# Attention with normed q and k, then a gated feed-forward net: rearranging the outset, the order of the weights' sums, and the place of three conversions

## The chip, the cores and the metric

The kernel runs on one core of one Trainium2 chip. The metric is the device time in microseconds (us) of one execution, given as the median of several. Besides that I use the trace of one profiled execution of each kernel: its instructions with start, duration and what ended the wait ahead of them, and the granted clock of TensorE.

## The reference

```python
# q, k, v: (8, 12, 448, 64) float32; w_gate, w_val: (768, 1536); w_out: (1536, 768)
def rmsnorm(x, g): return x / sqrt(mean(x * x, -1) + 1e-6) * g
scores = rmsnorm(q, g_q) @ rmsnorm(k, g_k).T / 8          # per head
attn   = softmax(scores) @ v                              # (8, 12, 448, 64)
x      = attn.transpose(0, 2, 1, 3).reshape(3584, 768)
xn     = rmsnorm(x, rms_g)
g      = xn @ w_gate
out    = (g * sigmoid(g) * (xn @ w_val)) @ w_out
```

## The kernel before

The kernel goes through 8 sequences of 6 pairs of heads. While the attention of one pair runs, TensorE's pauses are filled with products of the feed-forward net of the sequence before. Each head's 448 rows are 3 tiles of 128 and a "rest" of 64 rows; the rests of several pairs are normed together. From sequence 1 on, the weights are used in a Strassen form, which needs sums of weight blocks: 72 of one kind (`derive`) and some of a second kind (`derive_o`), all made on VectorE. In the first sequence the weights are converted (`convert`: each one goes through ScalarE, then VectorE, then GpSimd). Names in the traces: `tr` are transposes, `sc` scores, `e` exponentials, `den` denominators and `rd` their reciprocals, `av` products with v and `x` = `av` times `rd`, `rb` the reciprocal roots of x's rows spread over a bank, `ff` the feed-forward products, `p` and `u` copies and sums that empty their banks (a bank is a piece of the memory that TensorE writes to), `w` a block of weights or a sum of two (`top` in some places), `warm` products of the identity. In source order the emitter calls `pe(...)` for one step of TensorE; `after(n, ...)` puts work n steps later. Cuts are marked with `# ...`.

```python
def norm_rests(b, lo, hi):
    n = hi - lo
    rest = st["rest", b][:, lo:hi]
    # ... square on ScalarE, then after(1): row sums on VectorE into ms
    def scale():
        nc.gpsimd.tensor_scalar(ms, ms, D * 1e-6, None, ALU.add)
        nc.gpsimd.tensor_tensor(ms, ms, mhalf[...], ALU.pow)          # reciprocal roots
        nc.gpsimd.tensor_tensor(rest, rest, ms..., ALU.mult)
    after(1 if b == 0 else 2, scale)

def norm_q(g):                                                        # qn = q * rs
    for h in range(2):
        nc.gpsimd.tensor_tensor(qn..., st["qk", g]..., st["rs", g]..., ALU.mult)

def fill(n=None):
    # ... for each step of the feed-forward net that is due:
        while asked["derived"] < sums_made:      # a sum that this step needs
            derive(0)                            # ...
        pe(fn)
        convert()
        derive()
        derive()
        derive_o()

# the outset
squares(0, 0); warm(9)                           # warm(n): n products of the identity
norm_rests(0, 0, 1)                              # pair 0's rest
# ... turn(0, 1), squares of pair 1
warm(3)
pe(lambda: turn(0, 0))                           # transposes of q, and of the rest
norm_rests(0, 1, 3)                              # rests of pairs 1 and 2
# ... g == 0: scores of pair 0, squares of pair 2, turn(1, 0), turn(1, 1)
# ... each later pair of the first sequence: convert() in three slots
```

The exponentials of a pair are added up by GpSimd (`es`, for the denominators) soon after the pair's scores.

## Time and profile before

| | before |
|---|---|
| median (range), us | 1622.38 (1621.83 to 1622.67) |
| span of the profiled execution, us | 1619.2 |
| TensorE busy | 98% |
| TensorE idle in 0 to 20 / 320 to 460 / 460 to 1400 us | 8.8 / 8.6 / 1.3 |
| half clock (granted clock 0.5), us from the start | 19.6 to 26.4, 347.2 to 350.7, 449.6 to 453.1 |

TensorE is the bound; what a change can win is idle time of TensorE and time at half clock. The main lines stand in the prediction below. TensorE's waits in 85 to 103 us (engine, line, releaser: total us, how often, longest):

```profile
PE av L563 <- issue: 1.9, 1, 1.9
```

### The profile page before, as it was taken

Reading aid. Unit: us, or ns where it says so; the run is one execution under the profiler, and the core shown is the slowest. Engines: PE = TensorE matmul, PEld = TensorE weight load, DVE = VectorE, ACT = ScalarE, POOL = GpSimd, SP = SyncE. Lnnn points to the kernel's source line nnn. Section 1 sums busy time; section 2 is a strip of 40 time slices with the busy share of each in tenths; the row PEclk is TensorE's granted clock in tenths of the full one; section 3 lists DMA queues with packets and bytes.
Section 4 is the critical chain, followed back from the end, with each engine's and each line's share of the span. In section 5 each row is a group of like instructions: output and inputs, shape, how many; then the busy total and the mean of one; then the engine's idle time right before and its main releaser. Section 6 shows DMA issues by size and latency. Waiting matters only on the chain.

```text
span 1619.2 us, 21550 instructions
## 1 busy us (share of the span) xinstructions
PE 1587.8 (98%) x7328; PEld 1124.6 (69%) x7328; DVE 864.3 (53%) x1490; ACT 471.7 (29%) x944; POOL 649.3 (40%) x672
## 2 busy tenths in 40 slices
PE   7999999999999999999999999999999999999998
PEld 3344445677865888668875688758886588969974
DVE  4989899378852354425563354524565235433431
ACT  5746564223221232223222222222232123101110
POOL 6867877444523344324632444334443322100000
PEclk9999999999999999999999999999999999999999
DMA  6747574566665655575544655476454464557652
GB/s 190 220 137 251 173 237 138 188 196 223 199 221 162 187 147 156 158 222 153 154 142 132 195 153 160 118 224 186 141 156 127 147 181 114 153 187 234 173 144 58
DMA packets 264586, 276.81 MB, mean 171 GB/s; under 512 B 79124, under 2 KB 261396, under 8 KB 264468
## 3 DMA queue, kind: packets, MB, share of 16 engines
q1 hardware_dynamic: 263540, 275.15, 56.3%
q8 instruction: 60, 0.98, 0.3%
q14 instruction: 58, 0.48, 0.1%
q10 hardware_dynamic: 800, 0.20, 0.1%
q0 software_dynamic: 128, 0.00, 0.0%
HBM read 235.93 MB, written 39.32 MB: 170 GB/s over the span
## 4 chain that ended last, share of the span: by engine, by line
PE 80%; DVE 6%; issue 0%; ACT 0%; POOL 0%; DVEq 0%; ACTq 0%
PE ff L878 39%; PE ff L1076 21%; PE av L579 5%; PE sc L527 5%; PE ff L973 3%; PE sc L557 2%; PE den L592 2%; PE tr L511 1%; DVE rd L600 1%; DVE w L835 1%; DVE top L726 1%; DVE top L727 1%; PE ff L1107 0%; DVE w L855 0%; DVE top L725 0%
## 5 line engine op out<-in xcount | busy, mean ns | idle before, releaser
L878 PE MATMUL ff<-x,w 128*128 128x224 f32 x1704 | 350.6, 355 | 3.0 <-ACT p L911 3.0
L878 PEld LDWEIGHTS ff<-x,w 128*128 128x128 f32 x1704 | 321.3, 191 | 14.6 <-issue 5.9
L537 POOL TENSOR_TENSOR es<-e 128x448 f32<-128x448 f32 x82 | 91.3, 1134 | 525.5 <-ACT e L531 525.5
L878 PE MATMUL ff<-xs,w 128*128 128x224 f32 x1320 | 272.0, 354 | 1.0 <-DVE u L890 1.0
L878 PEld LDWEIGHTS ff<-xs,w 128*128 128x128 f32 x1320 | 248.7, 191 | 5.4 <-issue 3.9
L1076 PE MATMUL ff<-w,h 128*128 128x384 f32 x582 | 200.2, 487 | 0.0
L544 POOL TENSOR_TENSOR es<-es,e 64x448 f32<-64x448 f32 (+1 forms) x164 | 194.1, 1194 | 6.3
L600 DVE RECIPROCAL rd<-rd 128x448 f32<-128x448 f32 x41 | 121.0, 2952 | 126.6 <-ACT rd L599 126.5
L531 ACT ACTIVATE e<-sc,rs 128x448 f32<-128x448 f32 x288 | 161.6, 634 | 50.6 <-PE sc L527 48.7
L1076 PEld LDWEIGHTS ff<-w,h 128*128 128x128 f32 x582 | 109.0, 190 | 76.1 <-DMA vt<-in_v_dram 3.3
L527 PE MATMUL sc<-qT,kT 64*128 64x448 f32 x576 | 138.7, 575 | 3.4 <-DVE kT L517 2.1
L1076 PE MATMUL ff<-w,so 128*128 128x384 f32 x350 | 120.4, 488 | 2.0 <-DVE y L1037 2.0
L579 PE MATMUL av<-e,vt 128*64 128x448 f32 x576 | 119.3, 549 | 0.0
L490 POOL TENSOR_TENSOR rs<-ms,mhalf 128x12 f32<-128x12 f32 (+1 forms) x50 | 114.9, 2298 | 4.2
L527 PEld LDWEIGHTS sc<-qT,kT 64*128 64x128 f32 x576 | 54.4, 186 | 84.0 <-issue 68.3
L1107 PE MATMUL ff<-x,w 128*128 128x448 f32 x288 | 111.8, 541 | 0.0
L890 DVE TENSOR_TENSOR cc<-ff,u 128x448 f32<-128x448 f32 x84 | 52.3, 623 | 88.9 <-PE ff L878 88.8
L1076 PEld LDWEIGHTS ff<-w,so 128*128 128x128 f32 x350 | 65.5, 190 | 48.4 <-DVE y L1037 3.9
L763 POOL TENSOR_TENSOR w<-top,raw 128x384 int32<-128x384 int32 x72 | 77.0, 1083 | 39.4 <-DVE top L727 24.2
L579 PEld LDWEIGHTS av<-e,vt 128*64 128x64 f32 x576 | 37.2, 137 | 76.6 <-issue 75.9
L1107 PEld LDWEIGHTS ff<-x,w 128*128 128x128 f32 x288 | 53.3, 190 | 50.8 <-issue 49.0
L613 POOL TENSOR_TENSOR ss<-ss,rd 128x448 f32<-128x448 f32 x40 | 47.4, 1185 | 76.9 <-ACT rd L612 76.9
(122 smaller groups left out, 1912.8 us busy)
## 6 DMA issues: line engine op xcount, KB each, us to landing
w<-kept SPq DMA_DIRECT2D x477, 192.0 KB, 2.9
w<-kept_o SPq DMA_DIRECT2D x290, 192.0 KB, 2.8
kept<-w SPq DMA_DIRECT2D x86, 192.0 KB, 3.9
top<-kept SPq DMA_DIRECT2D x75, 192.0 KB, 2.5
qk<-in_q_dram SPq DMA_DIRECT2D x48, 192.0 KB, 2.9
qk<-in_k_dram SPq DMA_DIRECT2D x96, 96.0 KB, 3.3
vt<-in_v_dram SPq DMA_DIRECT2D x48, 192.0 KB, 2.5
raw<-in_moe_w_gate_dram SPq DMA_DIRECT2D x24, 384.0 KB, 4.6
```

The lines of the kernel that those rows point to most:

```text
L490: nc.gpsimd.tensor_tensor(st["rs", g][:, cols], ms, mhalf[:, cols], ALU.pow)
L527: nc.tensor.matmul(ps[:, 0:S], lhsT=kT[r, c * 128:(c + 1) * 128], rhs=qT[r, :], start=True, stop=True)
L531: nc.scalar.activation(e, ps[:, 0:S], ACT.Exp, scale=rs[:, n:n + 1])
L537: nc.gpsimd.tensor_tensor(es, st["e", g, 0, j], st["e", g, 1, j], ALU.add)
L544: nc.gpsimd.tensor_tensor(es[r], es[r], e[r], ALU.add)
L579: nc.tensor.matmul(av[own(j), 0:S], lhsT=vt[:, j, c], rhs=st["e", g, c, j], start=False, stop=(c == NK - 1), skip_group_check=True)
L600: nc.vector.reciprocal(rd, rd)
L763: nc.gpsimd.tensor_tensor(data(key).bitcast(I32), top, lo, ALU.add)
L878: nc.tensor.matmul(bank[:, w * HT:(w + 1) * HT], lhsT=wt[:, c * 128:(c + 1) * 128], rhs=x[:, c, :], start=onto is None and w == c == 0, st ...
L890: nc.vector.tensor_tensor(add[name], ps[:, 0:S], add[other], ALU.add)
L1076: nc.tensor.matmul(ps, lhsT=a, rhs=data(("wo", b, name, c)), start=first and c == 0, stop=c == NFP - 1, skip_group_check=True)
L1107: nc.tensor.matmul(bank[w][:, 0:S], lhsT=data(key)[:, c * 128:(c + 1) * 128], rhs=st["x", 0, half][:, c, :], start=half == c == 0, stop=ha ...
```

## The change

Its intent: in the outset, norm the rests of pairs 0 and 1 in one group, put q's scaling of the first two pairs and the first rest's on VectorE, and fill two pauses with seven more products of the identity so that the clock stays up; in sequence 1, hold the weights' sums back while GpSimd adds exponentials, then make up to five a step; in the last pair of the first sequence, move three conversions behind the denominators and the scores.

```diff
 def norm_rests(b, lo, hi):
+    first = b == lo == 0
     def root():  # add and pow on GpSimd
+    def scale():
+        (nc.vector if first else nc.gpsimd).tensor_tensor(rest, rest, ms..., ALU.mult)
+    after(1 if b == 0 else 2, root)
+    if first:
+        return scale
 def norm_q(g):
-            nc.gpsimd.tensor_tensor(qn...)
+            (nc.vector if g <= 1 else nc.gpsimd).tensor_tensor(qn...)
 def turn(g, i):                       # q: between its transposes and the rest's
+            if g == 0:
+                warm(5)
 def fill(n=None):
-            derive()
-            derive()
-            derive_o()
+            if now["t"] - st["block"] > 4:       # steps since the pair's scores
+                for _ in range(3):
+                    derive()
+                derive_o()
+                derive_o()
 # outset
-    norm_rests(0, 0, 1)
+    scale = norm_rests(0, 0, 2)
+    after(1, scale)                   # behind squares(0, 1)
-    warm(3)
+    warm(5)
-    norm_rests(0, 1, 3)
 # g == 0 (pair 1's transposes now around the squares of pair 2)
+            norm_rests(0, 2, 4)
 # pairs 1 to 6: the three slots for conversions
-            convert() / convert() / convert()
+            turns(g < NPAIR) / turns(g < NPAIR) / turns(1 if g < NPAIR else 3)
```

## The prediction

> **What bounds the kernel now.** I read the page's busy shares and slices, then the table of windows, the list of TensorE's waits, and the timeline around each wait.
>
> ```profile
> PE 1587.8 (98%) x7328; PEld 1124.6 (69%) x7328; DVE 864.3 (53%) x1490; ACT 471.7 (29%) x944; POOL 649.3 (40%) x672
> ...
> PE   7999999999999999999999999999999999999998
> ```
>
> TensorE is busy nearly everywhere; the comparison of instruction orders shows that the change leaves TensorE's order alone except for seven more identity products. So the change can only win back idle stretches and stretches of half clock. The table of windows (busy us by engine, then granted clock) says where these are:
>
> ```profile
> 0.00:20.00 20.00, 11.20 (x54) 7.47 (x54) 5.17 (x15) 10.77 (x21) 14.73 (x30) 0.99 0.80 216
> 19.00:27.00 8.00, 6.57 (x22) 1.96 (x24) 3.48 (x8) 3.79 (x9) 5.54 (x6) 0.57 0.45 115
> ...
> 320.00:460.00 140.00, 131.38 (x681) 108.85 (x680) 112.16 (x198) 36.68 (x73) 60.24 (x61) 0.98 0.67 217
> ...
> 460.00:1400.00 940.00, 938.70 (x4517) 698.21 (x4517) 430.34 (x757) 247.42 (x487) 350.50 (x358) 1.00 0.54 161
> ```
>
> From 460 on there is 1.3 us to win in 940, and the change touches nothing there. The outset has 8.8 us without a matmul in 20, followed by half clock (0.57 over 8 us, so about 6.9 us at half). Sequence 1's products, 320 to 460, have 8.6 us idle; narrow windows there show 0.57 over 347 to 351 and 0.66 over 449 to 454, which is 3.4 us at half each time. TensorE's own list of waits names the causes, first for 0 to 32, then for 320 to 460:
>
> ```profile
> PE tr L513 <- POOL rest L453: 4.2, 2, 3.2
> PE sc L527 <- DVE kT L517: 2.1, 1, 2.1
> ```
>
> ```profile
> PE ff L878 <- ACT p L911: 3.0, 1, 3.0
> PE ff L878 <- DVE u L890: 2.5, 2, 1.5
> PE tr L511 <- DVE kT L515: 2.0, 1, 2.0
> PE ff L878 <- DVE top L835: 1.1, 2, 0.8
> ```
>
> The timeline of 326 to 348 shows how the weights' sums (L835, L855) meet GpSimd's additions:
>
> ```profile
> 327.08 1.02 DVE L835 TENSOR_TENSOR w<-w,w 128x384 f32<-128x384 f32 x2
> ...
> 337.07 5.68 POOL L544 TENSOR_TENSOR es<-es,e 128x448 f32<-128x448 f32 x4
> ...
> 339.39 2.37 DVE L835 TENSOR_TENSOR w<-w,w 128x384 f32<-128x384 f32 x2
> ...
> 347.51 4.82 PE L878 MATMUL ff<-x,w 128*128 128x224 f32 x16 [3.02 <-ACT p L911]
> ```
>
> Two sums take 1.0 us alone and 2.4 us beside the additions; at 337.5 and 341.7 the second kind (L855) takes 1.48 us, not 0.55. VectorE reaches its row-of-squares sums only at 345.9, ScalarE's next square waits for those, its copy p stands behind the square, and TensorE waits for the copy.
>
> **What the Trainium skill says.** "SBUF — State Buffer", section "Who interferes with whom": a VectorE instruction with two SBUF inputs contends with a GpSimd one that reads SBUF. The trace agrees (0.5 against 1.2 to 1.5 us). "TensorE: Matmul & The Clock Gate", Part 1: an idle window of about 3.4 us puts the array at half rate, and it takes such a window of work to get it back. The trace agrees: the half-clock stretches are 3.4, 3.4 and about 6.9 us. "GPSIMD Engine Reference", section 4.1: elementwise work with two inputs belongs on VectorE, GpSimd being about twice as slow. "VectorE: DVE Perf Modes", the section on the TRN2 errata, gives (N + 151)/0.96 ns for an fp32 tensor_tensor: estimates of 357 ns for 192 elements and 424 for 256. For 128 and 384 it gives 291 and 557, and the trace has 0.28 and 0.55 us; GpSimd takes 0.97 us for the two 192s and 0.61 us for a 256.
>
> **The change, part by part.**
>
> *Outset, pair 0.* The two scalings of q go from GpSimd to VectorE: 0.97 us becomes about 0.6 (two of 357 ns, overlapping), so the transposes at 7.59 come some 0.3 earlier. The rest's chain gets longer, as it now handles two pairs: square 0.42 for 0.31, reduction 0.42 for 0.29 and behind the k copy on VectorE (about 0.4 more), power 1.04 for 0.72 (both sizes are rows of the timeline), product 0.42 for 0.40. That is +1.0, less a little overlap: the rest of pair 0 is transposed at about 10.0 instead of 9.18. **Loss 0.8.** The identity products fill this pause; each is two records of about 0.11 us at full clock, so the 2 + 5 added cost 1.5 us of TensorE, in time it would idle.
>
> *Outset, pair 1.* Here the rest was the bound: GpSimd worked through four powers of 1.35 us, one scaling, and then the second group's 0.23 + 1.04 + 0.61 up to 17.6. Now that rest is long done. The first pair's scores end at 14.9 (14.0 + 0.8), the transposes follow at once, ScalarE's qT can start after the six exponentials at about 16.2 and takes 0.63, VectorE's two copies 0.7: pair 1's first score starts at 17.6, not 20.43. **Gain 2.8.** TensorE's pause is then 15.3 to 17.6, 2.3 us, under the 3.4 us window, so the half clock of 6.9 us should vanish: **gain 3.** But the next group (pairs 2 and 3) is now scaled by GpSimd only after pair 2's q: sums of squares done at 18.9, power 2.46, scaling 0.97, then 0.25 + 1.04 + 0.61 puts the rest at 24.9, where TensorE would want it at 23.3. **Loss 1.6**, and this is the wait that takes the place of the one removed. The 0.8 is inside the 17.6. So pair 1's block ends some 3.7 us earlier than its 31.6: outset, 2.8 + 3.0 - 1.6, about **4** before friction, and I take **3.5**. GpSimd has 24 of 31 us in the next three pairs, so it keeps up.
>
> *Last pair of the first sequence.* The wait of 1.9 at 92 ("issue") is for the bank that VectorE's x (91.25 to 91.87) frees. One conversion leaves the stretch ahead of the reciprocal (1.25 us). But the denominators end at 87.4 and the reciprocal alone is 2.95, so it can start only 0.8 us sooner: **gain 0.8**. The three conversions behind it fall where VectorE has 6 us idle (4.2 busy of 11 from 92 to 103).
>
> *Sequence 1's sums.* Same instructions, 72 on VectorE, held until the fifth step after the scores, then up to five a step instead of three. Four pairs, from the order of VectorE before and after:
> - Pair at 330: all nine sums leave the stretch of additions; the 3.0 wait and its 3.4 us of half clock (1.7) go: +4.7. But six sums and two of the second kind then stand ahead of u, and four, not two, between the two u's: the product that needs the second bank could start at 351.9 and starts at about 354.3: -2.4. Net **+2.3**.
> - Pair at 366: three sums in place of four plus one ahead of the first u: 1.2 wait less 0.9, **+0.9**; the 0.8 wait for `top` is for a needed sum and stays.
> - Pair at 405: eight sums and two of the other kind in the free stretch before the two u's, where DVE was already the bound (1.5 at 423.6): about 1 worse, **-1**.
> - Pair at 434: no sum is left before the k copy; the 0.3 and 2.0 waits and 3.4 us of half clock go: **+4**.
>
> Sum +6.2; I take **6**.
>
> Altogether 3.5 + 0.8 + 6, some 10.3 of 1622.4: **1612.0 us**.
>
> **Rivals.**
> 1. *The sums only move the jam.* Bursts of five sums (2.5 us) on an engine that has its own evacuations every 2.27 us make TensorE wait for banks; then the pairs at 330 and 405 give back more, the part gives 1 to 2, and the time is about 1617. For it: VectorE is busy 112 of 140 us there and I find two such stalls by hand. Against: the contention removed is real VectorE time, some 0.7 us a sum for about twenty of them.
> 2. *The outset is paid back.* Data arrive no sooner: pair 3's q and k land at 22 to 22.7, the weights behind them, and from 63 to 92 GpSimd and VectorE (23.4 and 28.5 of 29.1 us) pace the loop. If VectorE is the true pace up to 100, the gain of the outset shrinks to 1 and the time is about 1614.5. Against: TensorE has no wait at all from 31.6 to 62.9.
> 3. *All waits go.* If the VectorE backlog clears better than my sums by hand, sequence 1 gives 11 and the outset 6: about 1604.
>
> **Range and chances.** I weigh my sum most, rivals 1 and 2 next, 3 least. A range of **1605.5 to 1618.5** should hold it 8 times in 10. 2% would be 32 us; all idle and half-clock time before 460 together is under 30, so faster than that has a chance of 0.01, within 2% 0.98, slower 0.01.
>
> **What would show it.** Right: pair 1's first score near 17.6; a granted clock of 1.0 from 19 to 27, and in 347 to 351 shifted; the rest of pair 2 waited for near 24; the pair at 330 with sums of 0.5 us, not 1.2; no wait for kT in sequence 1's last pair; from 460 on the same stream, shifted. Wrong: a half clock still after pair 1's pause, new waits of TensorE on u over 3 us in sequence 1, or a later part that is longer by what the earlier ones saved.

## The result, and the profile after

The changed kernel's median is 1614.2 us (1613.70 to 1614.41, 4 runs); the kernel before beside it 1622.41 us (4 runs). The ratio is 0.9949, 95% interval 0.9932 to 0.9967. (A ratio is the mean time of one kernel's fast runs over that of the other's of the same rounds, so not quite the ratio of the medians quoted.) That is 8.2 us less, where 10.4 was predicted: within 2%, and inside the range of 1605.5 to 1618.5.

The busy line of the changed kernel's page hardly differs from before, as TensorE does the same work:

```profile
PE 1584.4 (98%) x7342; PEld 1123.7 (70%) x7342; DVE 859.9 (53%) x1495; ACT 472.3 (29%) x944; POOL 645.8 (40%) x667
```

The table of windows of the changed kernel (start:end, length, then busy us and instructions of PE, PEld, DVE, ACT, POOL, then granted clock, DMA share, GB/s) answers the one in the prediction:

```profile
0.00:20.00 20.00, 14.49 (x72) 9.58 (x72) 6.72 (x20) 10.31 (x20) 11.09 (x22) 0.91 0.85 230
19.00:27.00 8.00, 6.76 (x39) 2.66 (x41) 3.74 (x10) 5.36 (x13) 6.50 (x9) 1.00 0.60 156
8.40:11.80 3.40, 1.63 (x10) 0.71 (x8) 1.33 (x5) 1.25 (x3) 2.92 (x4) 1.00 0.84 200
11.80:15.20 3.40, 3.40 (x10) 1.13 (x10) 1.09 (x3) 1.70 (x3) 2.02 (x4) 0.50 0.99 315
320.00:460.00 140.00, 133.13 (x703) 108.89 (x704) 111.76 (x213) 37.71 (x76) 58.69 (x61) 1.00 0.72 234
460.00:1400.00 940.00, 938.70 (x4525) 700.50 (x4526) 428.07 (x749) 247.73 (x487) 351.26 (x358) 1.00 0.55 159
```

The clock of 0.57 over 19 to 27 is 1.00, and sequence 1 has a clock of 1.00 and 1.75 us more of matmul in the same 140 us. New is a half clock at 11.8 to 15.2. From 460 on both kernels have 938.70 us of matmul in 940: nothing changed there.

TensorE's waits in 0 to 32 us of the changed kernel, then in 85 to 103, then in 320 to 460:

```profile
PE sc L537 <- ACT sq L478: 2.0, 1, 2.0
...
PE tr L523 <- POOL rest L458: 1.2, 1, 1.2
PE tr L523 <- DVE rest L458: 1.0, 1, 1.0
```

```profile
PE av L573 <- issue: 1.2, 1, 1.2
PE rb L649 <- POOL rs L641: 1.0, 1, 1.0
```

```profile
PE ff L888 <- DVE w L845: 4.0, 2, 2.5
PE ff L888 <- DVE u L900: 2.8, 2, 1.4
```

The waits for p, kT and `top` in sequence 1 are gone, 8.6 us with those for u before; in their place are 6.8 us of waits for needed sums (w, new) and for u. The timeline of the changed kernel shows why, in the pair that began at 330:

```profile
335.83 4.66 POOL L554 TENSOR_TENSOR es<-es,e 128x448 f32<-128x448 f32 x4
...
342.00 2.43 DVE L845 TENSOR_TENSOR w<-w,w 128x384 f32<-128x384 f32 x5
342.70 2.51 PE L888 MATMUL ff<-xs,w 128*128 128x224 f32 x12 [1.54 <-DVE w L845]
```

GpSimd's four additions take 4.66 us, not 5.68, and five sums 2.43 us, 0.49 each, where two beside the additions took 2.37. The contention is gone. But the first sum now starts at 342.0, and a product waited 1.54 us for it.

**Where the time went.** As TensorE's order is the same (the identity products aside), the same product can be followed through two traces: its start in one minus its start in the other is the lead gained so far. How much of a lead is the clock, I take from the granted clock's records: half of the difference in half-clock time up to there. That is an upper bound, as slow products in front of a wait cost less. The first profile of the changed kernel leads by 2.80 us at 45 us, 1.08 at 320 and 7.06 from 460 to the end. Half-clock time went from 13.65 to 3.41 us, so up to 5.12 of the 7.06 are the clock, and at least 1.9 are shorter waits.

### The profile page after: what moved, and what is told of

It reads as the page before. It is cut to its first block, busy times and chain, and to the rows that moved or that the text cites.

```text
span 1612.2 us, 21593 instructions
## 1 busy us (share of the span) xinstructions
PE 1584.4 (98%) x7342; PEld 1123.7 (70%) x7342; DVE 859.9 (53%) x1495; ACT 472.3 (29%) x944; POOL 645.8 (40%) x667
## 4 chain that ended last, share of the span: by engine, by line
PE 83%; DVE 4%; issue 0%; ACT 0%; DMA 0%; POOL 0%; DVEq 0%
PE ff L888 41%; PE ff L1086 22%; PE sc L537 6%; PE av L589 5%; PE ff L983 3%; PE sc L567 2%; PE den L602 2%; PE tr L519 1%; DVE top L736 1%; DVE top L737 1%; DVE rd L610 1%; PE ff L1117 0%; DVE top L735 0%; PE rb L649 0%; PE msx L637 0%
## 5 line engine op out<-in xcount | busy, mean ns | idle before, releaser
L888 PE MATMUL ff<-x,w 128*128 128x224 f32 x1740 | 354.2, 353 | 1.4 <-DVE u L900 1.4
L888 PEld LDWEIGHTS ff<-x,w 128*128 128x128 f32 x1740 | 326.5, 190 | 11.6 <-issue 4.6
L554 POOL TENSOR_TENSOR es<-es,e 64x448 f32<-64x448 f32 (+1 forms) x164 | 190.8, 1174 | 6.3
L1086 PE MATMUL ff<-w,so 128*128 128x384 f32 x338 | 116.1, 488 | 1.3 <-DVE y L1047 1.3
L1117 PEld LDWEIGHTS ff<-x,w 128*128 128x128 f32 x288 | 53.3, 190 | 50.8 <-issue 49.0
```

Of the source, the lines that this page charges most:

```text
L554: nc.gpsimd.tensor_tensor(es[r], es[r], e[r], ALU.add)
L888: nc.tensor.matmul(bank[:, w * HT:(w + 1) * HT], lhsT=wt[:, c * 128:(c + 1) * 128], rhs=x[:, c, :], start=onto is None and w == c == 0, st ...
L1086: nc.tensor.matmul(ps, lhsT=a, rhs=data(("wo", b, name, c)), start=first and c == 0, stop=c == NFP - 1, skip_group_check=True)
L1117: nc.tensor.matmul(bank[w][:, 0:S], lhsT=data(key)[:, c * 128:(c + 1) * 128], rhs=st["x", 0, half][:, c, :], start=half == c == 0, stop=ha ...
```

## The experiments

Twelve runs were made, eleven of new kernels and one of the changed kernel again, all correct. The first four ran on one chip (before there: median 1622.28, 1618.52 to 1623.85, 11 runs), the next four on another (before 1621.05, 1617.96 to 1622.10, 9 runs), the next three on a third (before 1622.05, 1617.60 to 1623.48, 11 runs), the last on a fourth (before 1621.10, 1617.89 to 1622.17, 9 runs). Kernels from different chips are better compared by their ratios than by their medians. The record also lists the mean granted clock of every single run, profiled or not, and within a kernel the slow runs are on the whole those with the lower clock: e1's go from 0.998 at 1616.74 us to 0.993 at 1623.98, those of the kernel before on the first chip from 0.996 at 1618.52 to 0.992 at 1623.85. A mean clock lower by 0.005 is some 16 us at half, an estimate of 8 us of time, so most of the scatter between runs can be half clock.

The leads over the first profile of the kernel before, by stretch of that kernel's time, in us; in brackets the part that the clock can account for at most, by its records:

| kernel | 0 to 45 | 45 to 320 | 320 to 460 | at the end |
|---|---|---|---|---|
| changed, first profile | +2.80 (1.71) | -1.72 | +5.98 (3.41) | 7.06 (5.12) |
| e1 outset only | +4.36 (3.41) | -1.33 | +1.52 (1.71) | 4.55 (5.12) |
| e2 conversions only | -0.08 | -0.52 | -2.67 (-3.41) | -3.27 (-3.41) |
| e3 sums only | +0.32 | -0.02 | +5.93 (3.41) | 6.23 (3.41) |
| e4 without conversions | +4.39 (3.41) | -1.33 | +5.98 (3.41) | 9.04 (6.82) |
| changed, again | +4.42 (3.41) | -1.66 | +5.93 (3.41) | 8.69 (6.82) |
| e5 no identity products | +2.77 (1.71) | -1.66 | +5.92 (3.41) | 7.03 (5.12) |
| e6 more identity products | +4.42 (3.41) | -1.25 | +4.26 (1.71) | 7.43 (5.12) |
| e8 hold, old rate | +4.42 (3.41) | -2.89 (-1.71) | +4.22 (1.71) | 5.75 (3.41) |
| e7 one sum while adding | +4.41 (3.41) | -1.35 | +7.80 (3.41) | 10.86 (6.82) |
| e9 three rests | +2.46 (0) | -2.23 (-1.71) | +4.25 (1.71) | 4.48 (0) |
| e10 = e6 and e7 | +4.39 (3.41) | -1.81 (-1.71) | +7.90 (3.41) | 10.48 (5.11) |
| e11 = e10, old rate | +4.29 (3.41) | -2.89 (-1.71) | +8.12 (3.41) | 9.52 (5.11) |

### The parts alone

**e1_outset_only**: the kernel before with the outset's part of the diff alone.

> The kernel before with the outset's part alone (grouped rests, scaling on VectorE, seven more identity products). Theory A, the parts add up as the two traces show when the same product is followed through both: at 27 us the lead is 2.9 us, by 65 us it is down to 1.6, and no more is lost: 1620.8 us. Rival B, the backlog of VectorE and GpSimd from 55 to 92 us sets the pace, so the lead is gone by 92 us unless conversions leave that stretch: 1622.2 us. Rival C, my prediction's sizes: 3.5 us kept, 1618.9.

Measured: median 1618.21 us (1616.74 to 1623.98, 6 runs), ratio 0.9987 [0.9971, 1.0002]. That is nearest rival C's number, but by time alone it is not told from no change, as the runs scatter by 7 us. Rival B fell in the trace: 3.0 us of the lead are still there at 320. The trace is clearer: pair 1's first score stands at 17.51 us (17.6 predicted), no half clock in the outset, a lead of 4.36 at 45. Sequence 1 is unchanged code here, and yet it was 1.52 us shorter than before: its half clock at 449 did not come. So the granted clock differs between runs of the same code.

**e2_conv_only**: the kernel before with the conversions' part alone.

```diff
-            convert()        # three slots of the pairs 1 to 6
+            turns(g < NPAIR) # slots 1 and 2
+            turns(1 if g < NPAIR else 3)   # slot 3
```

> The kernel before with only the conversions of the last pair of the first sequence moved behind its sums. Theory A (the traces of before and after: 0.7 us won at the wait for the value bank, 1.1 lost at the wait of the norm's broadcast for GpSimd's power behind the moved additions): 0.4 us slower, 1622.8. Rival B (it keeps VectorE from pacing the stretch): faster by 0.8, 1621.6. In the profile a wait of about 1 us of the rb products for GpSimd should be new.

Measured: median 1620.43 us (1617.41 to 1624.45, 6 runs), ratio 0.9989 [0.9973, 1.0005]: again not told apart by time, and under both expected numbers. Its trace has half clock at 347 and 449 for 6.8 us each, where the kernel before had 3.4, in code that neither changed; hence the -2.67 in its row. The part itself is in 45 to 320: -0.52, that is +0.69 at the bank (91.97), -1.10 at `rb` behind it, as in the changed kernel's waits above, and -0.11 in small steps.

**e3_sums_only**: the kernel before with the hold and the faster rate alone.

```diff
-            derive()
-            derive()
-            derive_o()
+            if now["t"] - st["block"] > 4:
+                for _ in range(3):
+                    derive()
+                derive_o()
+                derive_o()
```

> The kernel before with only the weights' sums held for four steps and then done faster. Theory A (parts add up): the 5.9 us that the traces give from 320 to 454 us, 1616.5. Rival: part of that came only because TensorE was ahead or because the clock's windows fell well; then 1618 or later. In the profile the half clock near 347 and 449 us should be gone, and two new waits of TensorE for a weights' sum, about 1.5 and 2.5 us, should be there.

Measured: median 1614.83 us (1614.07 to 1616.13, 5 runs), ratio 0.9958 [0.9946, 0.9971]. This is the part that shows in the time; it is under the 1616.5 of theory A. TensorE's waits in 320 to 460 are those of the changed kernel:

```profile
PE ff L878 <- DVE w L835: 4.0, 2, 2.5
PE ff L878 <- DVE u L890: 2.9, 2, 1.5
```

**e4_no_conv**: the changed kernel with one conversion in each slot, as before.

```diff
-            turns(g < NPAIR) / turns(g < NPAIR) / turns(1 if g < NPAIR else 3)
+            turns(1) / turns(1) / turns(1)
```

> The changed kernel with the conversions put back where they were. Theory A: 0.4 us faster than the changed kernel, 1613.8 against 1614.2. Rival B (the conversions' move is what lets the outset's lead live): 1 us slower than the changed kernel, 1615.2.

Measured: median 1613.88 us (1612.03 to 1615.24, 5 runs), ratio 0.9955 [0.9942, 0.9968]. Its profile has no half clock at all before the end. The leads of the parts, each in the stretch that it changes, add up: e1's 4.36 - 1.33 and e3's 5.93 make 8.96, e4 has 9.04.

### The clock, and the conversions once more

**c_after_again**: the changed kernel itself, as the control for the three below.

> The changed kernel once more, as the control for the kernels beside it. My theory (the parts add up; which pauses drop the clock depends on where the clock's windows of 3.4 us happen to lie in a run) expects a median of 1613.5 to 1615 us and a spread of 1.5 to 3 us between its runs. Rival (the chip decides, the phase does not): a spread under 0.5 us and another level. The place of the half clock in its profile (11.8 to 15.2 us before) may be another one.

Measured: median 1612.62 us (1612.37 to 1614.19, 5 runs), ratio 0.9954 [0.9940, 0.9967]; a little lower than I expected, with the spread as expected. Its profile has no half clock. The same window of the same kernel, now:

```profile
11.80:15.20 3.40, 3.40 (x19) 1.57 (x18) 1.09 (x3) 2.94 (x6) 2.02 (x4) 1.00 0.96 303
```

Nineteen matmul records against ten in 3.4 us. In the records the granted clock holds for multiples of 3.41 us, so I speak of clock windows of that length. The first profile's began at 5.0 us, this one's at 6.6. So the clock window ahead of the half clock was 8.4 to 11.8, with 1.63 us of matmul; this profile's, 6.57 to 9.98 and 9.98 to 13.39, have 2.80 and 2.69. The four other profiles with the same outset (e1, e4, e7, e8) have clock windows from 5.8 to 7.1 us, and no half clock in the outset either. Up to the end this profile is 1.64 us ahead of the first, of which 1.6 were gained by 15.3 us and kept. So a half clock of 3.41 us costs some 1.6 us, and the profiles fit that whether it comes depends on where the clock windows lie. What the outset gains there is not lost later.

It also shows what the conversions do, as neither e4's profile nor this one has half clock: against e4 the changed kernel is 0.76 us ahead behind the bank near 88 (0.69 of it won there) and loses 1.10 at `rb` near 96, in the end 0.35 us slower. That is too little to see in the medians. Why `rb` is late is in the timelines, of the kernel before and then of the changed kernel (first profile):

```profile
95.56 0.16 DVE L629 TENSOR_SCALAR ms<-msx 112x4 f32<-112x4 f32 x1 [2.43 <-PE msx L627]
```

```profile
96.36 0.15 DVE L639 TENSOR_SCALAR ms<-msx 112x4 f32<-112x4 f32 x1
96.60 1.02 POOL L641 TENSOR_TENSOR rs<-ms,mhalf 112x4 f32<-112x4 f32 x1 [0.96 <-DVE ms L639]
```

Before, VectorE sat idle until the sums of squares were there, and took its small step (L629) at once. In the changed kernel it is busy without a gap from 89.55 on, with the moved conversions: the parts of one that run beside GpSimd's take 1.30, 1.05 and 1.26 us, not 0.35, 0.36 and 0.56, and the small step stands behind them. GpSimd's root waits 0.96 us for it, and `rb` for the root.

**e5_no_identity**: the changed kernel without its seven added identity products.

```diff
-            if g == 0:
-                warm(5)
...
-    warm(5)
+    warm(3)
```

> The changed kernel without its seven added identity products. If those seven keep the clock up in the outset: the pause at 8.4 to 10 us is then empty, a window of 3.4 us there has under 1.5 us of matmul, half clock of 3.4 us or more appears near 10 to 15 us in most runs, and the median is 1 to 2 us above the changed kernel's (about 1615.5). If they do nothing (the pause is too short with or without them): same median within 0.5 us.

Measured: median 1615.29 us (1614.04 to 1616.63, 5 runs), ratio 0.9968 [0.9954, 0.9981], 2.7 above the control's median. The windows of e5 at the same place:

```profile
8.40:11.80 3.40, 1.17 (x5) 0.44 (x5) 1.33 (x5) 1.25 (x3) 2.91 (x4) 1.00 0.82 196
11.80:15.20 3.40, 3.40 (x10) 1.14 (x10) 1.09 (x3) 1.70 (x3) 2.02 (x4) 0.51 0.95 294
```

This is the first branch of the expectation by the medians, though 2.7 us is more than the 1 to 2 expected; the intervals of the two ratios overlap. The profiles alone don't decide it: e5's lead is 1.66 below the control's (8.69 against 7.03), one half clock, but its clock windows began at 5.1 us, and the first profile of the changed kernel, with windows from 5.0, has the same half clock and a lead of 7.06 in spite of the products. In the single runs, three of the control's five have a granted clock of 0.999, as its profile without half clock has, and none of e5's. So the seven products probably help in some runs; by the first profile, five and two are not always enough.

**e6_more_identity**: e4 with 11 more.

```diff
             if g == 0:
-                warm(5)
+                warm(8)
             # transpose of the rest
+            if g == 0:
+                warm(2)
...
             pe(lambda: turn(1, 1))
+            warm(6)
```

> The changed kernel with the conversions put back to one per slot, and with 11 more identity products in the outset: 8 rather than 5 ahead of the first rest's transpose, 2 behind it, 6 in the pause ahead of pair 1's first score. If the half clock at 11.8 us of the changed kernel is what made its outset worth 1.6 us less, no run of this kernel has half clock before 30 us, and the median falls by 0.5 to 1.5 us against the same kernel with fewer products (1613.9 measured before, so 1612.5 to 1613.4), with a spread under 2 us. Rival: the added products delay the rest's transpose or the scores (they are in order with them): +0.3 to +1 us.

Measured: median 1613.79 us (1613.61 to 1614.06, 5 runs), ratio 0.9957 [0.9943, 0.9970]. The spread of 0.45 us is under the expected 2, but the median did not fall. The outset did what it should, at 2.76 us of matmul in the window:

```profile
8.40:11.80 3.40, 2.76 (x20) 1.83 (x18) 1.33 (x5) 1.21 (x3) 2.91 (x4) 1.00 0.80 188
11.80:15.20 3.40, 3.40 (x19) 1.57 (x18) 1.09 (x3) 2.94 (x6) 2.02 (x4) 1.00 0.97 299
```

Yet its profile has a half clock at 410.7 to 414.1, behind the 2.5 us wait for a needed sum in the pair at 405; the lead in sequence 1 is 4.26 where it was 5.98. The rival (the added products delay the scores) fell too: the lead at 45 us is 4.42 as in the control. Only one run was profiled, but none of the five has a granted clock above 0.998, the profiled run's, where the control has 0.999 three times: so by the record each of them had some half clock, and why the median did not fall is answered in part. For the outset e6 and e10 say more than e5: with the 11 products and clock windows from 4.5 and 5.1 us neither has half clock there, where both profiles with fewer products and windows from 5.0 and 5.1 (the first one and e5's) have it.

### The hold

**e8_hold_old_rate**: e4, holding, but two sums and one a step afterwards, as before the change.

```diff
             if now["t"] - st["block"] > 4:
-                for _ in range(3):
-                    derive()
-                derive_o()
-                derive_o()
+                derive()
+                derive()
+                derive_o()
```

> The changed kernel with conversions at one per slot and with sums still held while GpSimd adds, but then at the old rate of two and one per step, not three and two. If the hold alone brings the gain and the bursts of five cause the new waits on u (1.4 us at 354, and the lost 1.1 of the pair at 405): the u waits go, but more sums are still due when a product needs one, so waits on needed sums grow by 1 to 3 us. I expect 1614 to 1616, slightly worse than with the faster rate (1613.9). If bursts are the main loss: 1612 to 1613.

Measured: median 1615.31 us (1612.31 to 1615.63, 5 runs), ratio 0.9959 [0.9946, 0.9973]. Its waits in 320 to 460:

```profile
PE ff L888 <- DVE w L845: 5.1, 4, 2.5
PE ff L888 <- DVE u L900: 0.6, 1, 0.6
PE tr L519 <- DVE kT L525: 0.4, 1, 0.4
```

As expected, u waits 0.6 instead of 2.8, and needed sums 5.1 instead of 4.0. The bursts do cause the waits on u; without them the backlog turns into waits elsewhere. Its profile also has two half clocks, at 89 and at 410 us, so its lead is not to be compared with e4's as a whole.

**e7_one_while_adding**: e4, letting one sum per step through while GpSimd adds.

```diff
             if now["t"] - st["block"] > 4:
                 # three derive(), two derive_o()
+            else:
+                derive()
```

> The changed kernel with conversions at one per slot, and with one weights' sum per step let through while GpSimd adds, in place of none. Theory: the two new waits of TensorE for a needed sum (1.5 us near 341, 2.5 us near 410) come from the hold being too strict: VectorE idles some 4 us there. Then three or four sums run at 1.2 us each inside the additions, both waits go, sequence 1 is 3 to 4 us shorter, and the median is 1609.5 to 1611.5 against 1612 to 1614 with the full hold. Rival (any sum beside the additions brings the jam back: additions of 5.7 us again, u and p late): the waits for sums go and waits for u or p of the same size come, 1613 to 1615.

Measured: median 1611.37 us (1610.12 to 1614.37, 6 runs), ratio 0.9942 [0.9928, 0.9956]. The timeline of e7 in the same pair, and its waits in 320 to 460:

```profile
334.02 5.17 POOL L554 TENSOR_TENSOR es<-es,e 128x448 f32<-128x448 f32 x4
...
337.04 1.16 DVE L845 TENSOR_TENSOR w<-w,w 128x384 f32<-128x384 f32 x1
```

```profile
PE ff L888 <- DVE u L900: 3.8, 3, 2.2
PE ff L888 <- DVE w L845: 1.0, 1, 1.0
```

A sum beside the additions takes 1.16 us, over twice its time, and the additions 5.17 for 4.66: the contention is back in part. But VectorE idled in that stretch anyway, so it costs nothing that ends late, and the sum needed at 341 is there. The waits for needed sums fall from 4.0 to 1.0; 1.0 comes back as u (2.8 to 3.8). Sequence 1's lead is 7.80, not 5.98. The theory held, with about half the size expected.

### Other tries

**e9_three_rests**: e4 with the rests of three pairs in the first group.

```diff
-    scale = norm_rests(0, 0, 2)
+    scale = norm_rests(0, 0, 3)
-            norm_rests(0, 2, 4)
+            norm_rests(0, 3, 4)
```

> The changed kernel with conversions at one per slot, and with the first three pairs' rests in the first group, not two. Pair 2's wait for its rest (1.2 us near 24) goes; the first rest comes 0.4 to 0.6 us later (power of six 1.35 in place of 1.04, product 0.56 in place of 0.43). If TensorE is the pace of the outset, its lead at 30 us grows by 0.7 and stays: median 0.7 lower (1612.5 to 1613.3). If VectorE and GpSimd pace 50 to 100 us (my second rival), the lead is gone again by 65 us, and the median is the same within 0.4. The longer first pause may also drop the clock more often (+1.6).

Measured: median 1614.70 us (1613.12 to 1616.57, 6 runs), ratio 0.9956 [0.9943, 0.9969]. Pair 2's wait for its rest is gone, and the first rest's wait is 1.6 us. But the longer pause dropped the clock for 6.9 us:

```profile
7.60:11.00 3.40, 1.61 (x13) 1.23 (x11) 1.72 (x6) 1.26 (x4) 2.59 (x4) 1.00 0.80 209
11.00:17.90 6.90, 6.35 (x16) 1.98 (x16) 1.77 (x5) 3.17 (x6) 4.15 (x5) 0.51 1.02 310
```

So at 45 us it leads by 2.46, not by 5. It is no better, and it tells something about my second rival: behind e4 by 1.93 at 45 us, it is still 2.8 behind at 320, with one more half clock in between. That difference, made in the outset, stays.

**e10_identity_and_one**: e6 and e7 together.

> Both remedies: more identity products in the outset, and one sum per step while GpSimd adds. If the half clocks come from the outset's pauses and the waits for needed sums, none is left before the end, so the spread is under 1 us and the median 1609 to 1610.5. If the waits only move: 1612 to 1614 with half clock in sequence 1.

Measured: median 1611.14 us (1610.05 to 1611.78, 6 runs), ratio 0.9938 [0.9924, 0.9951]. That misses the expected 1609 to 1610.5, and the spread is 1.7 us, not under 1: its profile has a new half clock at 76.8 to 80.2, where VectorE, ScalarE and GpSimd are all full:

```profile
73.40:76.80 3.40, 2.02 (x8) 0.86 (x7) 3.37 (x3) 3.40 (x8) 3.32 (x4) 1.00 1.02 327
76.80:80.20 3.40, 3.40 (x17) 1.62 (x17) 3.26 (x7) 3.36 (x8) 2.06 (x3) 0.50 0.47 106
```

**e11_one_then_old_rate**: e10, with two sums and one a step after the hold.

> The kernel with both remedies (more identity products, one sum per step beside GpSimd's additions), but with the old rate of two sums and one of the second kind once the additions are over, not three and two. Left in it are waits on u of 2.1 us near 351 and 1.4 us near 370. If the bursts of five make those: the first falls to about 0.8, no wait on a needed sum comes back as the backlog is smaller, and the median is 1609.5 to 1610.5 (1611.1 measured with bursts). If without bursts the sums come late again: waits on needed sums of 1 to 3 us in the pairs at 405 and 434, median 1612 to 1614.

Measured: median 1610.18 us (1609.82 to 1611.52, 5 runs), ratio 0.9936 [0.9922, 0.9950]: the fastest of all, though its interval is not apart from e10's. The median is as expected. The wait on u of 2.1 us near 351 is gone (no wait on u is over 0.6), so the bursts made it; against the expectation some waits for needed sums came back, 2.1 us in three places instead of 1.0 in one, none over 1.0. Its profile has one half clock, at 89 us; two of its other runs have a granted clock of 1.000. It is the kernel before with the changed outset, more identity products and a limit of one sum per step beside GpSimd's additions; the bursts and the moved conversions are not needed. By time alone it is not shown to beat the changed kernel, whose control has 0.9954 [0.9940, 0.9967]; the profiles' leads are 9.5 to 10.9 us for e7, e10 and e11, and 7.1 and 8.7 for the changed kernel.

## Why the prediction was right, and where not

The time was in the range, 2.2 us above the middle. By the prediction's own steps:

- **Pair 0's rest at about 10.0**: 9.90. Right.
- **Pair 1's first score at 17.6**: 17.51 in e1, but 19.07 in the first profile. The working was right; the difference is the half clock at 11.8. The prediction checked one pause against 3.4 us, "TensorE's pause is then 15.3 to 17.6", and not the one around pair 0's rest, whose window had only 1.63 us of matmul. That cost 1.6 of the outset's gain in that profile: the step that failed in the outset.
- **Half clock of 19 to 27 gone, gain 3**: right; the records give up to 3.41. **Pair 2's rest, loss 1.6**: the wait is 1.2. The terms shown for "24.9" add up to 24.2, and in e4, without half clock, the rest was done at 24.15. Where the clock stayed up, the outset led by 4.4 at 45 us, against 4 by the sum.
- **The outset is paid back (rival 2)**: right in part, mechanism included. Every kernel with the new outset and the rests of two pairs in its first group loses about 1.3 us between 53 and 65 us (0.45 and 0.8), whether it leads by 2.8 (the first profile) or by 4.4 (e4). No run was made on it, but the timelines, before and then of the changed kernel's first profile, show where VectorE falls behind:

```profile
56.87 0.36 DVE L726 TENSOR_SCALAR top<-top 128x384 int32<-128x384 int32 x1
```

```profile
54.12 1.03 POOL L458 TENSOR_TENSOR rest<-rest,msr 128x384 f32<-128x384 f32 x1
...
54.49 0.87 DVE L736 TENSOR_SCALAR top<-top 128x384 int32<-128x384 int32 x1
```

  This part of a conversion now runs beside GpSimd's product of the rests, which came after it before. With the two parts like it that are slower too, VectorE reaches its next sums of squares 0.82 us later, measured by its own lead (3.95 to 3.13 in e4, 2.37 to 1.55 in the first profile). ScalarE's square waits 2.67 us for them instead of 1.26, its exponentials stand behind, and TensorE's scores at 64 (times of the kernel before) wait for banks. The 0.45 at 57 are VectorE's too: there the products `av` start 0.15 us after VectorE's `x` in both kernels, and `x` was only 3.95 ahead in e4, where TensorE was 4.39. So VectorE paces these two places. The prediction's "TensorE has no wait at all from 31.6 to 62.9" was true but no proof of slack: VectorE was busy 29.95 of those 31.30 us. What rival 2 had wrong is the amount, as all but 1.3 of the lead stays. That the time came out so near its 1614.5 is luck.
- **Conversions, gain 0.8**: the step whose working failed. The wait for the bank shrank by 0.7 as worked out. "The three conversions behind it fall where VectorE has 6 us idle" counted VectorE's idle time and not what it was waiting for in it: its small step towards the reciprocal roots of x. The conversions, up to three times as long beside GpSimd's, fill the time in front of that step, which comes at 96.36 although the changed kernel was ahead; TensorE then waits 1.0 us. In place of +0.8 the part is worth -0.35.
- **Sequence 1's sums, gain 6**: 5.98, 5.93 and 5.93 in three profiles. The sum is right, partly by luck, as its errors cancel. The pair at 405 loses 1.1, as said, but to a needed sum that comes 2.5 us late, not at u. The pair at 330 gives 1.4, not 2.3: u cost 1.6 instead of 2.4, and 1.7 were lost to a wait of the other kind (1.54 for a needed sum). For these two pairs the prediction counted what VectorE must do ahead of u and did not ask when each product needs its sum. The pair at 366 gave the 0.9 predicted, the pair at 434 4.8 instead of 4.
- **The sums only move the jam (rival 1)**: by waits this is nearly what happened: 8.6 us of waits became 6.8. What made it worth 6 us is in large part that the two half clocks went, up to 3.41 of the 5.98; the new waits are all shorter than 3 us and spread out.

Of the 10.3 predicted, the conversions (0.8 predicted, -0.35 found), the loss at 53 to 65 (1.3, foreseen only in the rival) and the half clock in the outset (1.6, in some runs) are what was missing. Against them stand up to 0.9 more from the outset before that loss.

## What to carry to other kernels

Where TensorE is the bound, weigh a pause by the clock it drops as well as by its length: two pauses of the same sum can differ by 1.6 us for each window of half clock, so spreading waits out, or filling them with idle products, can be worth more than shortening them. When work is held back to avoid contention, ask when its results are needed, and let through as much as the contended engine can take in its own idle time. Before moving work "into an engine's idle time", ask what the engine waits for there and what will then stand behind the moved work, and take the work's length beside what the other engines do at that time. And that TensorE shows no wait in a stretch doesn't mean that the other engines have slack in it.

## What the Trainium skill lacked or had wrong

- "TensorE: Matmul & The Clock Gate", Part 1, says that the clock falls after an idle window of about 3.4 us, that the window is free-running, and that the cold count differs from run to run. The runs agree on the window (half clocks of 3.4 and 6.8 us) and on its free running. What the page lacks is how little work makes a window count as idle. No window ahead of a half clock in the table's stretches was wholly idle: half clock followed windows of 3.4 us with 1.17 (e5), 1.63 (changed kernel) and 2.02 us (e10) of matmul, by the trace's modelled ends. Busy time alone gives no clean threshold: e7 kept its full clock after a window with as little as 1.62. (The window of e10 holds only transposes and products on 64 rows, that of e7 only products on 128 rows; whether that matters, no run tested.) The windows of e7:

```profile
347.20:350.60 3.40, 1.62 (x9) 1.27 (x7) 3.30 (x7) 0.00 (x0) 2.13 (x4) 1.00 0.56 192
350.60:354.00 3.40, 2.99 (x16) 3.00 (x17) 2.45 (x6) 0.00 (x0) 0.00 (x0) 1.00 0.93 267
```

The page also advises not to fit a particular count of cold products, as the ramp is under 1% of a typical kernel. The size here agrees, but a change of 0.5% can drown in it: unchanged code of sequence 1 had 3.4, 6.8 and 13.7 us of half clock in three profiles (e1, before, e2), up to some 5 us of time, and the kernel before ran from 1617.6 to 1623.5 us on one chip. A single profile can't rank two kernels that are 3 us apart.
- "SBUF — State Buffer", section "Who interferes with whom", has the contention right but no size for this pair. Here a VectorE sum of two blocks of 128x384 took 1.16 us instead of 0.55 beside GpSimd's additions, and four of those took 5.68 us (three sums or more beside them) or 5.17 (one a step) instead of 4.66.
